# Splitting the spectrum straight from its PSUM bank, shrinking in the bank of the mix, and moving the lower part of y to GpSimd

## The chip, the cores and the metric

The kernel runs on one core of a Trainium2 chip. The metric is device time in microseconds of one execution; the table below gives the runs of the kernel before, and one further execution was taken with the profiler. Engines are named as in the profile: PE is TensorE (matmuls) and PEld its weight loads, DVE is VectorE, ACT is ScalarE, POOL is GpSimd, SP is SyncE, which here issues the DMAs.

## The reference, cut to what matters

```
X  = rfft(x, axis=1)                       # x: 8 x 3008 x 256
Yr = Xr @ w_r - Xi @ w_i + b_r
Yi = Xr @ w_i + Xi @ w_r + b_i
Yr, Yi = sign(Y) * max(|Y| - 0.01, 0)      # soft shrink, each part
y  = irfft(Yr + 1j*Yi, n=3008, axis=1)
g  = y @ w_gate; h = g * sigmoid(g) * (y @ w_val)   # 256 -> 1536
out = h @ w_out                                      # 1536 -> 256, 24064 rows
```

## The kernel before, in words

The kernel has two stages. `transform` does the Fourier transform, the complex mix of the channels, the shrink and the inverse transform for 8 batches; `gated_ffn` does the gated feed-forward net over 24064 rows in 24 blocks.

The transform of 3008 points is factored into 47 x 64. `stage_a` (L290 to L302) is the length-47 part: a chunk of x times the constant `wa`, copied out of PSUM by ACT (L298) and stored to DRAM as `d1`; there are 16 chunks to a batch. `stage_b` (L304 to L320) is the length-64 part for a pair p of the 24 rows k1 that are computed, 12 pairs to a batch and 96 in all: it loads `a_in` from `d1`, makes the spectrum in the PSUM bank `ps_b` (L311), and gives it to the mix as two parts. Every fp32 operand of the products in question is split into an upper part `hi`, rounded to the type `fp32r` of the matmuls, and a lower part `lo`, what is left of it; the list `PASSES` multiplies hi*hi, hi*lo and lo*hi. In `stage_b` ACT copies the bank to the tile `f` (real and imaginary part, L315), POOL adds the two as a third column block (L316), DVE rounds all three to `f_hi` (L318) and subtracts to get `f_lo` (L319).

`stage_mix` (L322 to L356) does the complex product with three real products: six matmuls of the sum go to the bank `ps_s` (L329), DVE adds them and the bias into the bank `mixb` of this pair (L331), and twelve more matmuls accumulate on that bank (L337). There are two `mixb` banks, used in turn. Then ACT copies the bank to the tile `t` in four pieces, which also moves the real and imaginary half to other partitions (L349), DVE clamps t to plus and minus 0.01 (L350), POOL subtracts that from t (L351), ACT rounds to `y_hi` (L354) and DVE makes `y_lo` (L355). `stage_bi` (L358 to L373) is the length-64 inverse: three matmuls into `ps_z` (L365, L368), an ACT copy to `z` (L370) and a store to `d2`. `stage_ai` (L382 to L396) is the length-47 inverse, four columns m at a time, into the banks `ps_x0` and `ps_x1`, copied by ACT (L395) and stored to `xt_d`. `load_seven` and `load_weights` (L213 to L257) turn the weights of the net into the seven operands of a Strassen-like scheme, on DVE, POOL and ACT, between the other work.

All eight PSUM banks are in use, one buffer to each name: `ps_a`, `ps_b`, `ps_s`, `ps_z`, `ps_x0`, `ps_x1` and the two `mixb`.

The order of the work comes from slots. The kernel puts a step of the work in a numbered slot with `at` and emits the slots in turn:

```
            at(s, lambda b=b, p=p: fs.__setitem__((b, p), stage_b(b, p)))
            at(s + 1, lambda b=b, p=p: ys.__setitem__((b, p), stage_mix(b, p, fs.pop((b, p)))))
            at(s + 2, lambda b=b, p=p: stage_bi(b, p, ys.pop((b, p))))
```

with s the running number of the pair. The order emitted is a priority only: a planner in the framework, which simulates the program with a cost for each instruction, fixes the queue of every engine when the program is built, and each engine then takes its queue strictly in that order. Loads are bound by `paced` to come after the newest load of `a_in` on SP. At the end of the transform's 96 pairs the net begins: `x_sum` (L500, POOL, four differences for the block) and `x_part` (L506, ACT rounds to the upper part, POOL subtracts for the lower) prepare block 0, and from there the order of the net is written out by hand and not planned.

Of the kernel before, what the change touches and what calls it, by code (L numbers as in the profile page):

```python
# [145 lines left out]
def transform(ctx, tc, front, last, ps_, xp, w_r, w_i, cb, wup_raw, wdn_raw, ca, cf, ci, co, wdn, wup_d, xt_d, d2):  # L146
# [143 lines left out]
    def stage_a(b, ch, xt):  # L290
        if ch == 0:
            d1[b] = dram.tile([NK, P, C], F32, name="d1", tag="d1")
        tag = "absz"[ch % 4] if b == 0 else "a"
        ps = ps_.tile([P, T], F32, name="ps_a", tag="ps_" + tag)
        nc.tensor.matmul(ps[:96], lhsT=wa, rhs=xt, start=True, stop=True)
        tag = "azt"[ch % 3] if b == 0 else "a"
        a = sb.tile([96, T], F32, name="a", tag=tag)
        nc.scalar.copy(a, ps[:96])  # L298
        store = nc.sync.dma_start(d1[b].rearrange("k (q m) c -> (k q) (m c)", m=NM)[:, ch * T : (ch + 1) * T], a)
        if b == 0 and ch == NCH - 1:  # L300
            gates.append(store)


    def stage_b(b, p):  # L304
        t = sb.tile([P, 2, C], F32, name="a_in", tag="a_in", bufs=3)
        gates.append(nc.sync.dma_start(t, d1[b][2 * p : 2 * p + 2].rearrange("k p c -> p k c")))
        ps = ps_.tile([P, T], F32, name="ps_b")
        for cc in range(2):
            for k in range(2):
                s = (cc * 2 + k) * P  # L310
                nc.tensor.matmul(ps[:, s : s + P], lhsT=t[:, k, cc * P : (cc + 1) * P], rhs=wf[:, 2 * p + k, :], start=True, stop=True)  # L311
        f = sb.tile([P, 3 * C], F32, name="f", tag="f", bufs=2)
        hi = sb.tile([P, 3, 2, P], F32R, name="f_hi", tag="f_hi")
        lo = sb.tile([P, 3, 2, P], F32R, name="f_lo", tag="f_lo")
        nc.scalar.copy(f[:, : 2 * C].rearrange("p (q a b) -> p a q b", q=2, b=64), ps.rearrange("p (a q b) -> p a q b", q=2, b=64))  # L315
        nc.gpsimd.tensor_tensor(f[:, 2 * C :], f[:, :C], f[:, C : 2 * C], op=ALU.add)  # L316
        flat = lambda x: x.rearrange("p q a b -> p (q a b)")
        v.tensor_copy(flat(hi), f)  # L318
        v.tensor_tensor(flat(lo), f, f32(flat(hi)), op=ALU.subtract)  # L319
        return hi, lo  # L320

    def stage_mix(b, p, parts):  # L322

        mixb = mixed[p % 2]
        p1 = ps_.tile([P, T], F32, name="ps_s")
# [1 line left out]
        for cc in range(2):  # L327
# [3 lines left out]
        v.tensor_tensor(  # L331
            mixb.rearrange("p (a c) -> p a c", c=C), p1[:, :C].rearrange("p (a c) -> p a c", a=1).to_broadcast([P, 2, C]), bias[0], op=ALU.add
        )
        for half, (q, i) in enumerate(((1, 2), (0, 1))):
            for cc in range(2):
                for w, x in PASSES:
                    nc.tensor.matmul(  # L337
                        mixb[:, half * C : (half + 1) * C],
                        lhsT=parts[x][:, q, cc, :],
                        rhs=wmix[i][w][:, cc, :],  # L340
                        start=False,
                        stop=(cc, w) == (1, 1),
                        skip_group_check=True,
                    )
        t = sb.tile([P, T], F32, name="t", tag="t", bufs=2)
        y = sb.tile([P, T], F32, name="y", tag="y", bufs=2)
        for k in range(2):
            for half in range(2):
                nc.scalar.copy(t[64 * half : 64 * half + 64, k * C : (k + 1) * C], mixb[64 * k : 64 * k + 64, half * C : (half + 1) * C])  # L349
        v.tensor_scalar(y, t, LAM, -LAM, op0=ALU.min, op1=ALU.max)  # L350
        nc.gpsimd.tensor_tensor(t, t, y, op=ALU.subtract)  # L351
        hi = sb.tile([P, T], F32R, name="y_hi", tag="y_hi")
        lo = sb.tile([P, T], F32R, name="y_lo", tag="y_lo")
        nc.scalar.copy(hi, t)  # L354
        v.tensor_tensor(lo, t, f32(hi), op=ALU.subtract)  # L355
        return hi, lo  # L356

    def stage_bi(b, p, parts):  # L358
# [52 lines left out]
    for b in range(B):  # L411
        base = NP * b
        for p in range(NP):
            s = base + p
            at(s, lambda b=b, p=p: fs.__setitem__((b, p), stage_b(b, p)))
            at(s + 1, lambda b=b, p=p: ys.__setitem__((b, p), stage_mix(b, p, fs.pop((b, p)))))
            at(s + 2, lambda b=b, p=p: stage_bi(b, p, ys.pop((b, p))))
    for k in range((B - 1) * NCH):
        b, ch = k // NCH + 1, k % NCH
        s = k / X_RATE if k < X_FAST else X_FAST / X_RATE + (k - X_FAST) * (X_END - LEAD - X_FAST / X_RATE) / ((B - 1) * NCH - X_FAST)  # L420
# [24 lines left out]
    paced(load_mix)  # L445
    paced(load_inverse)
    for s in sorted(slots):
        if s < B * NP + 2:
            for fn in slots[s]:
                fn()  # L450
        gates += stores
# [1 line left out]

    def finish():
        for s in sorted(slots):
            if s >= B * NP + 2:
                for fn in slots[s]:
                    fn()

# [3 lines left out]
def gated_ffn(ctx, tc, front, ring, ps_, co, wdn, wup_d, xt_d, d2, out):  # L463
# [33 lines left out]
            at += n  # L497
        xs[blk] = {}

    def x_sum(blk, o, a, b):  # L500
        f = lambda i: raws[blk][:, i, :]
        g.tensor_tensor(f(o), f(a), f(b), op=ALU.subtract)

    SUMS = ((4, 0, 1), (6, 2, 4), (5, 2, 0), (7, 3, 6))

    def x_part(blk, n_):  # L506
        h = BLOCKS[blk][1]
        src = raws[blk][:, X_AT[n_], :]
        part = xs[blk][n_] = sb.tile([P, 2, T], F32R, name="x_parts", bufs=12)
        act.copy(part[:, 0, :h], src)  # L510
        g.tensor_tensor(part[:, 1, :h], src, f32(part[:, 0, :h]), op=ALU.subtract)  # L511

    def product(o, weights, parts, start, stop):

# [222 lines left out]
    load_x(0)  # L737
    for k in range(RING - 1):
        load_unit(k)
    for sums_ in SUMS:  # L740
        x_sum(0, *sums_)
    for n_ in X_AT:
        x_part(0, n_)

    nc.tensor.matmul(b3, lhsT=wdn[0][:, 0, 0, :], rhs=xs[0][1][:, 0, :], start=True, stop=True)
    yield
# [72 lines left out]
```

## Time and profile before

| | us |
|---|---|
| runs: median (lowest to highest of 3) | 2745.8 (2737.93 to 2747.36) |
| profiled execution, whole | 2740.56 |
| its span, first to last instruction | 2738.8 |
| PE busy in the span | 2655.4 (97%) |
| DVE, ACT, POOL busy in the span | 2087.3, 1712.2, 2061.7 |

The span is 1.8 us shorter than the profiled execution. The first 42 us load x and do `stage_a` of batch 0, from 42 to 672 us the transform is in its steady course, 672 to about 692 us is the passage to the net, and the rest is the net. A busy PE in these tables has the latency of a matmul in it (a 128x256 product is listed at some 0.28 us while they follow one another every 0.12 us), so idle PE time is a lower bound of what a stall costs. A row of a group of instructions has its line, engine, operation, tile names and shapes, its count, its busy time and mean, and behind it the idle time of its engine just before these instructions with what ended that idle time.

### The profile page before, as it was taken

To read this page: it belongs to the slowest core of one execution; us is meant where nothing else is said; L and a number is where in the kernel's file an instruction comes from. 1 tells how busy PE (TensorE), PEld (TensorE's weight loads), DVE (VectorE), ACT (ScalarE), POOL (GpSimd) and SP (SyncE) were. 2 spreads that over 40 slices of the span, in tenths; PEclk is the share of its full clock that TensorE was granted. 3 is DMA by queue.
4 is the path that set the end of the run, shared out by engine and by line. 5 is a ranking of instruction groups with operands and counts; after the bars stand their busy time and mean duration, and the time that the engine had idled before them with its cause. 6 is when DMAs were issued, how large, how long until landed. Compare 5 with 4: busy or idle time off the path is not lost. (4 is left out here: it accounts for less than half of the span.)

```text
span 2738.8 us, 39634 instructions
## 1 busy us (share of the span) xinstructions
PE 2655.4 (97%) x13173; PEld 2207.0 (81%) x13173; DVE 2087.3 (76%) x2916; ACT 1712.2 (63%) x3280; POOL 2061.7 (75%) x1574
## 2 busy tenths in 40 slices
PE   8989998989999999999999999999999999999998
PEld 5777787778788888888888888888888888888898
DVE  3776677775778777887787877787778877888787
ACT  4666666666566666666666666666665666666665
POOL 1454465564888888888888888888888888888885
PEclk9999999999999999999999999999999999999999
DMA  8889898766354444444454444444454444444453
GB/s 251 256 271 294 283 293 267 229 197 203 137 172 156 156 141 164 168 155 157 140 171 161 150 156 149 170 156 157 140 172 156 162 144 146 154 164 153 146 185 105
DMA packets 180124, 491.88 MB, mean 180 GB/s; under 512 B 17264, under 2 KB 89584, under 8 KB 179824
## 3 DMA queue, kind: packets, MB, share of 16 engines
q1 hardware_dynamic: 179920, 489.35, 54.0%
q8 instruction: 105, 1.72, 0.3%
q14 instruction: 99, 0.81, 0.1%
HBM read 378.65 MB, written 110.62 MB: 179 GB/s over the span
## 5 line engine op out<-in xcount | busy, mean ns | idle before, releaser
L516 PE MATMUL bank<-x_parts,wup 128*128 128x512 f32 (+1 forms) x6048 | 1518.2, 386 | 1.2 <-POOL x_parts L511 0.7
L516 PEld LDWEIGHTS bank<-x_parts,wup 128*128 128x128 f32 x6048 | 1125.8, 188 | 226.5 <-DVE bank L645 5.4
L536 POOL TENSOR_TENSOR h_parts<-more,h_parts 128x512 fp32r<-128x512 f32 (+1 forms) x573 | 847.6, 1492 | 113.9 <-ACT h_parts L532 99.8
L536 POOL TENSOR_TENSOR h_parts<-hidden,h_parts 128x512 fp32r<-128x512 f32 (+1 forms) x432 | 565.1, 1316 | 204.0 <-ACT h_parts L532 164.5
L516 PE MATMUL bank<-h_parts,wdn_hi 128*128 128x512 f32 (+1 forms) x2016 | 613.5, 385 | 0.9 <-POOL h_parts L536 0.9
L532 ACT CAST h_parts<-hidden 128x512 fp32r<-128x512 f32 (+1 forms) x432 | 265.0, 613 | 451.3 <-DVE hidden L618 451.3
L516 PEld LDWEIGHTS bank<-h_parts,wdn_hi 128*128 128x128 f32 x2016 | 378.2, 188 | 74.1 <-POOL h_parts L536 1.8
L618 DVE TENSOR_TENSOR hidden<-hidden,bank 128x512 f32<-128x512 f32 (+1 forms) x576 | 376.0, 674 | 77.6 <-PE bank L516 69.2
L557 DVE TENSOR_TENSOR sums<-sums,bank 128x512 f32<-128x512 f32 (+1 forms) x360 | 241.9, 672 | 245.1 <-PE bank L516 245.1
L516 PE MATMUL bank<-h_parts,wdn_lo 128*128 128x512 f32 (+1 forms) x1008 | 388.6, 386 | 4.2 <-DVE sums L557 4.2
L532 ACT CAST h_parts<-more 128x512 fp32r<-128x512 f32 (+1 forms) x576 | 351.4, 610 | 41.8 <-DVE more L527 31.3
L616 ACT ACTIVATE hidden<-bank 128x512 f32<-128x512 f32 (+1 forms) x432 | 252.2, 584 | 117.6 <-PE bank L516 117.2
L527 DVE TENSOR_TENSOR more<-hidden 128x512 f32<-128x512 f32 (+1 forms) x288 | 293.0, 1056 | 0.0
L527 DVE TENSOR_TENSOR more<-hidden,more 128x512 f32<-128x512 f32 (+1 forms) x288 | 258.6, 898 | 0.0
L351 POOL TENSOR_TENSOR t<-t,y 128x512 f32<-128x512 f32 x96 | 133.4, 1389 | 136.6 <-DVE y L350 136.6
L645 DVE TENSOR_TENSOR bank<-hidden,bank 128x512 f32<-128x512 f32 (+1 forms) x288 | 197.0, 684 | 45.0 <-PE bank L516 32.2
L623 ACT COPY bank<-bank 128x512 f32<-128x512 f32 (+1 forms) x288 | 161.6, 561 | 109.4 <-DVE hidden L618 104.0
L516 PEld LDWEIGHTS bank<-h_parts,wdn_lo 128*128 128x128 f32 x1008 | 189.5, 188 | 40.8 <-issue 4.5
L511 POOL TENSOR_TENSOR x_parts<-xf,x_parts 128x512 fp32r<-128x512 f32 (+1 forms) x168 | 209.9, 1268 | 11.5 <-PE bank L516 7.1
L316 POOL TENSOR_TENSOR f<-f 128x256 f32<-128x256 f32 x96 | 85.3, 889 | 146.0 <-ACT f L315 142.9
L631 ACT COPY hidden<-bank 128x512 f32<-128x512 f32 (+1 forms) x288 | 167.6, 582 | 2.6
L349 ACT COPY t<-mixb 64x256 f32<-64x256 f32 x384 | 140.6, 366 | 29.6 <-PE mixb L337 20.1
(94 smaller groups left out, 3273.3 us busy)
## 6 DMA issues: line engine op xcount, KB each, us to landing
wup<-wup_d SPq DMA_DIRECT2D x288, 896.0 KB, 4.6
d<-a SPq DMA_DIRECT2D x128, 192.0 KB, 4.2
a_in<-d SPq DMA_DIRECT2D x96, 256.0 KB, 4.5
out<-o SPq DMA_DIRECT2D x88, 256.0 KB, 6.1
scratch<-xp SPq DMA_DIRECT2D x116, 192.0 KB, 4.6
d<-z SPq DMA_DIRECT2D x84, 256.0 KB, 3.8
z_in<-d SPq DMA_DIRECT2D x56, 384.0 KB, 5.1
xt_d<-xt SPq DMA_DIRECT2D x56, 376.0 KB, 4.4
```

The lines of the kernel that those rows point to most:

```text
L349: nc.scalar.copy(t[64 * half : 64 * half + 64, k * C : (k + 1) * C], mixb[64 * k : 64 * k + 64, half * C : (half + 1) * C])
L511: g.tensor_tensor(part[:, 1, :h], src, f32(part[:, 0, :h]), op=ALU.subtract)
L516: nc.tensor.matmul(o, lhsT=weights[w], rhs=parts[x], start=start and i == 0, stop=stop and i == 2, skip_group_check=True)
L527: v.tensor_tensor(at(o, h), at(a, h), at(b, h), op=ALU.subtract)
L532: act.copy(pair[i][:, 0, :h], at(i, h))
L536: eng.tensor_tensor(pair[i][:, 1, :h], at(i, h), f32(pair[i][:, 0, :h]), op=ALU.subtract)
L557: v.tensor_tensor(o, o, spare[:, :h], op=ALU.add)
L616: act.activation(at(i, h), src, AF.Silu)
L618: v.tensor_tensor(at(i, h), at(i, h), src, op=ALU.mult)
L623: act.copy(b3[:, :h], b1[:, :h])
L631: act.copy(m5, b2[:, :h])
L645: v.tensor_tensor(b2[:, :h], m5, b3[:, :h], op=ALU.add)
```

## The change

In `stage_b` the upper part of the spectrum is rounded by ACT from the bank itself, DVE subtracts it from the bank for the lower part, the sum of real and imaginary part is made by an ACT copy of one and a DVE addition of the other out of the bank (tile `f`, now 256 columns), and ACT and DVE split that sum. POOL's addition is gone. `f_hi` and `f_lo` have three buffers in place of two. `stage_mix` is cut in two: `stage_sum` has the six matmuls of the sum and the addition of the bias, one slot after `stage_b`; `stage_mix` has the twelve matmuls and the shrink, one slot later, and `stage_bi` follows one slot later again. DVE clamps and subtracts in the bank `mixb`, ACT copies the shrunk result out and rounds it, and POOL makes `y_lo`. For batch 0 `stage_a` takes six names of tiles with two buffers each in place of three. Before the net, block 0's differences are made by DVE, the first part's split is emitted ahead of them, and DVE makes three of the seven lower parts.

```diff
--- before.py
+++ after.py
@@ -293,7 +293,7 @@
         tag = "absz"[ch % 4] if b == 0 else "a"
         ps = ps_.tile([P, T], F32, name="ps_a", tag="ps_" + tag)
         nc.tensor.matmul(ps[:96], lhsT=wa, rhs=xt, start=True, stop=True)
-        tag = "azt"[ch % 3] if b == 0 else "a"
+        tag = ("a", "z", "t", "y", "y_hi", "y_lo")[ch % 6] if b == 0 else "a"
         a = sb.tile([96, T], F32, name="a", tag=tag)
         nc.scalar.copy(a, ps[:96])
         store = nc.sync.dma_start(d1[b].rearrange("k (q m) c -> (k q) (m c)", m=NM)[:, ch * T : (ch + 1) * T], a)
@@ -309,17 +309,23 @@
             for k in range(2):
                 s = (cc * 2 + k) * P
                 nc.tensor.matmul(ps[:, s : s + P], lhsT=t[:, k, cc * P : (cc + 1) * P], rhs=wf[:, 2 * p + k, :], start=True, stop=True)
-        f = sb.tile([P, 3 * C], F32, name="f", tag="f", bufs=2)
-        hi = sb.tile([P, 3, 2, P], F32R, name="f_hi", tag="f_hi")
-        lo = sb.tile([P, 3, 2, P], F32R, name="f_lo", tag="f_lo")
-        nc.scalar.copy(f[:, : 2 * C].rearrange("p (q a b) -> p a q b", q=2, b=64), ps.rearrange("p (a q b) -> p a q b", q=2, b=64))
-        nc.gpsimd.tensor_tensor(f[:, 2 * C :], f[:, :C], f[:, C : 2 * C], op=ALU.add)
-        flat = lambda x: x.rearrange("p q a b -> p (q a b)")
-        v.tensor_copy(flat(hi), f)
-        v.tensor_tensor(flat(lo), f, f32(flat(hi)), op=ALU.subtract)
+
+        total = sb.tile([P, 2 * P], F32, name="f", tag="f", bufs=2)
+        hi = sb.tile([P, 3, 2, P], F32R, name="f_hi", tag="f_hi", bufs=3)
+        lo = sb.tile([P, 3, 2, P], F32R, name="f_lo", tag="f_lo", bufs=3)
+        both = ps.rearrange("p (a q b) -> p a q b", q=2, b=64)
+        first = lambda x: x[:, :2].rearrange("p q c (k b) -> p (c k) q b", b=64)
+        blocks = lambda x: x.rearrange("p (a b) -> p a b", b=64)
+        flat = lambda x: x[:, 2].rearrange("p c a -> p (c a)")
+        nc.scalar.copy(first(hi), both)
+        nc.scalar.copy(blocks(total), both[:, :, 0])
+        v.tensor_tensor(blocks(total), blocks(total), both[:, :, 1], op=ALU.add)
+        v.tensor_tensor(first(lo), both, f32(first(hi)), op=ALU.subtract)
+        nc.scalar.copy(flat(hi), total)
+        v.tensor_tensor(flat(lo), total, f32(flat(hi)), op=ALU.subtract)
         return hi, lo
 
-    def stage_mix(b, p, parts):
+    def stage_sum(b, p, parts):
 
         mixb = mixed[p % 2]
         p1 = ps_.tile([P, T], F32, name="ps_s")
@@ -331,6 +337,11 @@
         v.tensor_tensor(
             mixb.rearrange("p (a c) -> p a c", c=C), p1[:, :C].rearrange("p (a c) -> p a c", a=1).to_broadcast([P, 2, C]), bias[0], op=ALU.add
         )
+        return parts
+
+    def stage_mix(b, p, parts):
+
+        mixb = mixed[p % 2]
         for half, (q, i) in enumerate(((1, 2), (0, 1))):
             for cc in range(2):
                 for w, x in PASSES:
@@ -344,15 +355,15 @@
                     )
         t = sb.tile([P, T], F32, name="t", tag="t", bufs=2)
         y = sb.tile([P, T], F32, name="y", tag="y", bufs=2)
+        v.tensor_scalar(y, mixb, LAM, -LAM, op0=ALU.min, op1=ALU.max)
+        v.tensor_tensor(mixb, mixb, y, op=ALU.subtract)
         for k in range(2):
             for half in range(2):
                 nc.scalar.copy(t[64 * half : 64 * half + 64, k * C : (k + 1) * C], mixb[64 * k : 64 * k + 64, half * C : (half + 1) * C])
-        v.tensor_scalar(y, t, LAM, -LAM, op0=ALU.min, op1=ALU.max)
-        nc.gpsimd.tensor_tensor(t, t, y, op=ALU.subtract)
         hi = sb.tile([P, T], F32R, name="y_hi", tag="y_hi")
         lo = sb.tile([P, T], F32R, name="y_lo", tag="y_lo")
         nc.scalar.copy(hi, t)
-        v.tensor_tensor(lo, t, f32(hi), op=ALU.subtract)
+        nc.gpsimd.tensor_tensor(lo, t, f32(hi), op=ALU.subtract)
         return hi, lo
 
     def stage_bi(b, p, parts):
@@ -413,8 +424,9 @@
         for p in range(NP):
             s = base + p
             at(s, lambda b=b, p=p: fs.__setitem__((b, p), stage_b(b, p)))
-            at(s + 1, lambda b=b, p=p: ys.__setitem__((b, p), stage_mix(b, p, fs.pop((b, p)))))
-            at(s + 2, lambda b=b, p=p: stage_bi(b, p, ys.pop((b, p))))
+            at(s + 1, lambda b=b, p=p: fs.__setitem__((b, p), stage_sum(b, p, fs.pop((b, p)))))
+            at(s + 2, lambda b=b, p=p: ys.__setitem__((b, p), stage_mix(b, p, fs.pop((b, p)))))
+            at(s + 3, lambda b=b, p=p: stage_bi(b, p, ys.pop((b, p))))
     for k in range((B - 1) * NCH):
         b, ch = k // NCH + 1, k % NCH
         s = k / X_RATE if k < X_FAST else X_FAST / X_RATE + (k - X_FAST) * (X_END - LEAD - X_FAST / X_RATE) / ((B - 1) * NCH - X_FAST)
@@ -445,7 +457,7 @@
     paced(load_mix)
     paced(load_inverse)
     for s in sorted(slots):
-        if s < B * NP + 2:
+        if s < B * NP + 3:
             for fn in slots[s]:
                 fn()
         gates += stores
@@ -453,7 +465,7 @@
 
     def finish():
         for s in sorted(slots):
-            if s >= B * NP + 2:
+            if s >= B * NP + 3:
                 for fn in slots[s]:
                     fn()
 
@@ -497,18 +509,18 @@
             at += n
         xs[blk] = {}
 
-    def x_sum(blk, o, a, b):
+    def x_sum(blk, o, a, b, eng=g):
         f = lambda i: raws[blk][:, i, :]
-        g.tensor_tensor(f(o), f(a), f(b), op=ALU.subtract)
+        eng.tensor_tensor(f(o), f(a), f(b), op=ALU.subtract)
 
     SUMS = ((4, 0, 1), (6, 2, 4), (5, 2, 0), (7, 3, 6))
 
-    def x_part(blk, n_):
+    def x_part(blk, n_, eng=g):
         h = BLOCKS[blk][1]
         src = raws[blk][:, X_AT[n_], :]
         part = xs[blk][n_] = sb.tile([P, 2, T], F32R, name="x_parts", bufs=12)
         act.copy(part[:, 0, :h], src)
-        g.tensor_tensor(part[:, 1, :h], src, f32(part[:, 0, :h]), op=ALU.subtract)
+        eng.tensor_tensor(part[:, 1, :h], src, f32(part[:, 0, :h]), op=ALU.subtract)
 
     def product(o, weights, parts, start, stop):
 
@@ -737,10 +749,12 @@
     load_x(0)
     for k in range(RING - 1):
         load_unit(k)
+
+    x_part(0, 1)
     for sums_ in SUMS:
-        x_sum(0, *sums_)
-    for n_ in X_AT:
-        x_part(0, n_)
+        x_sum(0, *sums_, eng=v)
+    for n_ in list(X_AT)[1:]:
+        x_part(0, n_, v if n_ in (6, 7, 4) else g)
 
     nc.tensor.matmul(b3, lhsT=wdn[0][:, 0, 0, :], rhs=xs[0][1][:, 0, :], start=True, stop=True)
     yield
```

## Rows read from the trace of the kernel before

**Rows 1.** The page, part 1: busy time, share of the span, instructions.
```profile
PE 2655.4 (97%) x13173; PEld 2207.0 (81%) x13173; DVE 2087.3 (76%) x2916; ACT 1712.2 (63%) x3280; POOL 2061.7 (75%) x1574
```

**Rows 2.** Stages: length, then busy PE PEld DVE ACT POOL, PEclk, DMA share, GB/s.
```profile
42.00:672.00 630.00, 576.94 (x3892) 487.15 (x3891) 445.96 (x618) 411.94 (x903) 336.11 (x301) 0.98 0.80 258
350.00:400.00 50.00, 48.44 (x334) 41.00 (x333) 37.23 (x54) 34.17 (x77) 25.11 (x23) 1.00 0.94 306
```

**Rows 3.** Waits of PE and PEld, 42 to 672 us: total us, times, longest.
```profile
PE mixb L337 <- DVE mixb L331: 18.7, 22, 2.1
PE ps_z L368 <- DVE y_lo L355: 8.7, 9, 3.0
PE ps_a L295 <- ACT a L298: 6.0, 7, 3.1
PE ps_z L368 <- ACT y_hi L354: 4.1, 5, 1.6
...
PEld mixb L337 <- DVE mixb L331: 33.0, 32, 2.6
```

**Rows 4.** Timeline near 403 us: start, length, instruction.
```profile
402.92 0.28 PE L329 MATMUL ps_s<-wm_lo,f_hi 128*128 128x256 f32 x1
...
406.38 0.69 DVE L331 TENSOR_TENSOR mixb<-ps_s,bias 128x512 f32<-128x512 f32 x1
```

**Rows 5.** Groups of DVE instructions by line, 42 to 672 us.
```profile
L319 DVE TENSOR_TENSOR f_lo<-f,f_hi 128x768 fp32r<-128x768 f32 x95 | 106.5, 1121 | 1.4
L355 DVE TENSOR_TENSOR y_lo<-t,y_hi 128x512 fp32r<-128x512 f32 x94 | 78.4, 835 | 93.2 <-ACT y_hi L354 93.2
L318 DVE CAST f_hi<-f 128x768 fp32r<-128x768 f32 x94 | 75.4, 802 | 53.1 <-PE mixb L337 51.2 <-POOL f L316 1.9
L350 DVE TENSOR_SCALAR y<-t 128x512 f32<-128x512 f32 x95 | 54.7, 576 | 4.7 <-ACT t L349 4.6
```

**Rows 6.** The same lines and L331 one by one: ns min/median/max.
```profile
L319 DVE TENSOR_TENSOR f_lo<-f,f_hi x95: 942/957/2830, 41.9 to 664.8; 128x768 fp32r<-128x768 f32 x95
...
L355 DVE TENSOR_TENSOR y_lo<-t,y_hi x94: 675/692/2586, 49.9 to 668.2; 128x512 fp32r<-128x512 f32 x94
...
L318 DVE CAST f_hi<-f x94: 546/561/1893, 45.1 to 663.6; 128x768 fp32r<-128x768 f32 x94
...
L350 DVE TENSOR_SCALAR y<-t x95: 408/420/2328, 46.6 to 669.8; 128x512 f32<-128x512 f32 x95
...
L331 DVE TENSOR_TENSOR mixb<-ps_s,bias x96: 684/691/700, 41.3 to 669.2; 128x512 f32<-128x512 f32 x96
```

**Rows 7.** Groups of ACT instructions and their waits, 42 to 672 us.
```profile
L354 ACT CAST y_hi<-t 128x512 fp32r<-128x512 f32 x95 | 59.0, 621 | 58.9 <-POOL t L351 58.5
...
L315 ACT COPY f<-ps_b 128x512 f32<-128x512 f32 x94 | 55.1, 587 | 60.3 <-DVE f_lo L319 52.1 <-PE ps_b L311 4.4 <-PE ps_x L388 1.6
...
L349 ACT COPY t<-mixb 64x256 f32<-64x256 f32 x380 | 139.2, 366 | 29.2 <-PE mixb L337 19.8 <-ACT z L370 2.0 <-issue 2.0
```

**Rows 8.** Groups whose durations serve as prices, whole span.
```profile
L645 DVE TENSOR_TENSOR bank<-hidden,bank 128x512 f32<-128x512 f32 (+1 forms) x288 | 197.0, 684 | 45.0 <-PE bank L516 32.2
...
L211 DVE TENSOR_TENSOR wi_lo<-raw_i,wi_hi 128x256 fp32r<-128x256 f32 x1 | 0.4, 424 | 0.2 <-ACT wi_hi L210 0.2
...
L210 ACT CAST wi_hi<-raw_i 128x256 fp32r<-128x256 f32 x1 | 0.4, 404 | 2.9 <-DMA raw_i<-ci 2.9
```

**Rows 9.** Groups of POOL instructions, 42 to 672 us.
```profile
L351 POOL TENSOR_TENSOR t<-t,y 128x512 f32<-128x512 f32 x95 | 132.1, 1391 | 133.5 <-DVE y L350 133.5
...
L316 POOL TENSOR_TENSOR f<-f 128x256 f32<-128x256 f32 x94 | 83.8, 892 | 107.9 <-ACT f L315 104.8 <-DVE y L350 3.0
```

**Rows 10.** Timeline of the first stage: ACT's copies in stage_a of batch 0.
```profile
18.83 2.52 ACT L298 COPY a<-ps_a 96x512 f32<-96x512 f32 x5 [4.77 <-DMA d<-a]
```

**Rows 11.** Timeline of the passage to the net: the seven lower parts.
```profile
679.90 8.72 POOL L511 TENSOR_TENSOR x_parts<-xf,x_parts 128x512 fp32r<-128x512 f32 x7 [3.87 <-ACT x_parts L510]
```

**Rows 12.** One stage of the passage, columns as in rows 2.
```profile
676.70:684.00 7.30, 5.91 (x12) 3.23 (x13) 0.69 (x1) 5.22 (x10) 4.10 (x4) 0.55 0.19 63
```

## The prediction

> **What bounds the kernel now.** I read the page first, then the busy times by stage, then the waits of PE, then the groups of DVE and ACT inside the transform, and last the timeline at both ends of it. Over the whole span PE is busy for 97% [rows 1], so only what is left between its products can be won. Nearly all of that lies in the transform: from 42 to 672 us PE is busy for 576.9 of 630 us [rows 2], which leaves 53.1 us idle, or 0.55 us for each of the 96 pairs of 6.56 us. No other engine is full there: DVE 446 us (71%), ACT 412 (65%), POOL 336 (53%), and the DMA engines have a share of 0.80, though 0.94 between 350 and 400 us.
>
> The waits say what ends PE's idle time. The largest is the mix waiting for the bias that DVE adds into its bank: 18.7 us as PE shows it, 33.0 as its weight loads show it, which can't run ahead either [rows 3]. The inverse waits 8.7 us for `y_lo` and 4.1 for `y_hi`, and `stage_a` 6.0 for ACT. The timeline shows why the bias is late. The products of the sum have started by 402.92 and the last takes 0.28 us, but DVE adds the bias only at 406.38 [rows 4]: some 3.2 us in which DVE's queue did other things first. That queue holds it up twice. In one place DVE waits: 93.2 us for `y_hi` before `y_lo`, and 51.2 us for the mix to have finished reading before `f_hi` overwrites its buffer [rows 5]. In the other its own instructions take longer than they need: the four lines that the change touches have means of 1121, 835, 802 and 576 ns [rows 5], but medians of 957, 692, 561 and 420 and maxima of 1.9 to 2.8 us, while the addition of the bias, which reads a bank of PSUM, always takes 684 to 700 ns [rows 6]. The difference of means and medians is 0.70 us for a pair, 68 us in all, and it comes at random, in queues whose order is fixed.
>
> The Trainium skill, page "SBUF — State Buffer", section "Who interferes with whom", says that a DVE instruction with at most one SBUF input outside the two-port modes does not contend with GpSimd, and that one with two SBUF inputs or in such a mode does. By that rule the trace agrees: the four lines spread up to fivefold and the bias line does not.
>
> **The change, part by part.** DVE: each pair loses f_hi, f_lo, the clamp and y_lo, 3.33 us by the means [rows 5], 2.63 by the medians [rows 6]. It gains five instructions. The lower part of 512 columns out of the bank and the clamp out of the bank I price at 0.69 us each (the bias line [rows 6]), the subtraction in the bank at 0.68 (L645), the addition and the lower part of 256 columns at 0.42 each (L211) [rows 8]: 2.91 us. By the means that is 0.42 us less for a pair, 40 us of DVE time over 96 pairs; by the medians 0.28 us more, 27 us in all. I take the means, because the time now lost to the spread is in the execution and only one short instruction of the new five (the 256-column lower part) reads two SBUF tiles.
>
> The Trainium skill, page "VectorE: DVE Perf Modes", section "Why PSUM operands drop a tier", speaks against the change: an operand in PSUM caps an fp32 instruction at one element a cycle, while the clamp in SBUF may run at two. The medians bear that out (420 ns for the clamp, 691 for the bias out of PSUM), and by it alone DVE would get slower by those 27 us rather than faster by 40.
>
> ACT: the copy of the whole bank stays (587 ns [rows 7]), and two instructions of 256 columns are added, 404 ns each by the nearest row [rows 8], 0.81 us for a pair and 78 us in all. ACT goes from 412 to 490 us, 78% of the stage: off the path on average, but it also empties `ps_a`, `ps_z` and `ps_x`, so I let the 6.0 us that PE waits for it double: +6. ACT also loses two waits of its own, 58.5 us for POOL's `t` and 52.1 for the buffer of `f` [rows 7].
>
> POOL: it loses 1.39 and 0.89 us for a pair [rows 9] and gains `y_lo` at about 1.25 (8.72 over seven [rows 11]): 1.0 us less. POOL is not on the path; its worth is that it disturbs DVE less.
>
> The split of the mix: the bias is now due a slot (6.56 us) ahead of the twelve products, and neither `y_lo` nor the wait for `y_hi` stands ahead of it on DVE. Its wait costs between 18.7 and 33.0 us [rows 3]; I take the weight loads' figure, as a product needs its load, and leave 4: -29. What I cover it with is the slot; without it, the 0.69 us of the bias is on the path again. What is queued behind the bias on DVE is the spectrum's split of the next pair. The bank `mixb` is held a slot longer, but there are two, and from the bias to the end of the copies I count a slot, clamp, subtraction and copies (6.56 + 0.69 + 0.68 + 1.46 = 9.4 us) and the products, of the 13.1 that two pairs give.
>
> From mix to inverse the chain was four copies at 366 ns, clamp 576, POOL 1391, rounding 621 and y_lo 835 [rows 5, 7, 9], 4.9 us; it becomes clamp 691, subtraction 684, copies, rounding and 1.25 us on POOL: 4.7. Its length stays; what goes is that y_lo stands in DVE's queue. Of the 12.8 us of `y_lo` and `y_hi` I take 8 off.
>
> The bank `ps_b` was freed by one ACT copy (587 ns); now ACT's two and DVE's two have to be done, 587 + 404 + 424 + 691 = 2.1 us with no queueing. The next pair needs it a pair's 6.56 us later, less its own eight products. From nothing to 0.5 us a pair (48 us) I take +3, near the low end, since the copy alone already starts late without stopping PE for it.
>
> Batch 0: ACT waits 4.77 us for a store to free a buffer [rows 10]. Twice the buffers remove that wait; the copies behind it still have to be made and stored on the same queue. Between 0 and -4.8 I take -2. SP's queue keeps its order: stores and then loads.
>
> The passage: POOL makes the seven lower parts in 8.72 us [rows 11] while PE waits for them; with three on DVE it needs four, 3.7 us less. From 676.7 to 684 us PE's granted clock is 0.55, near its lower level of 1.2 GHz, [rows 12]; its products then take longer than the parts need, so a little of it is lost: -3. The four differences (earlier, out of PE's way) count nothing. One slot more at the end: the chain of the last pair is as long as before, but with less beside it: +2.
>
> **Sum.** -29 - 8 + 6 + 3 - 2 - 3 + 2 = -31 us against the profiled execution's 2740.6: 2709.6, so **2710 us**. The median of the runs is 5.2 above that execution; I don't carry this over, as the runs themselves differ by 9.4. The net after 692 us is unchanged: same queues, written out by hand.
>
> **Rivals.**
> *The wait only changes its name* (no change). Slots are priorities and the planner has already put the sum's products 3.5 us ahead of the bias [rows 4], so the split may give it little that is new; DVE's time goes up by the medians, ACT's to 78%, and PE waits for ACT's copies of `a`, `z` and the spectrum as long as it did for the bias. For it: ACT would become the fullest engine after PE. Against it: 145 us of waits in DVE's queue and 110 in ACT's have their cause removed. Time: -29 and -8 are given back by ACT, only the start, the passage and the drain are left: about 2738. Chance 0.18.
> *The bank of the spectrum* (slower). With four readers on two engines, `ps_b` comes free too late as soon as the queueing of ACT and DVE between them comes near 6.56 - 2.1 = 4.4 us; DVE's lower part behind a long instruction of the weights can do that. If PE then waits 0.6 us for every pair, that is +58 on -31: about 2767. Chance 0.09.
> *All idle time goes.* If DVE's queue was behind all of PE's waits, the 53.1 us go, and the 4.8 at the start: about 2683. Against it: the DMA share of 0.94 where PE is already busy for 48.4 of 50 us [rows 2]; that part can't give much. Chance 0.11.
> *The change does not do what it says* can hardly be: the instructions are moved by name from one engine to another.
>
> **How the numbers follow.** The forecast itself gets 0.62. About 0.5% (13.7 us) is what a measurement of this kernel can tell from no change. The forecast's terms are good for about 12 us each way, so nearly all of it and the third rival count as faster: 0.71. The first rival and the forecast's weak end give 0.20 for the same, the second 0.09 for slower. The range reaches from the third rival, 2684, to just beyond the first, 2742; the second lies outside.
>
> **What would show it.** Right: in the steady stage, PE's wait for L331 near nothing, PE idle under 30 us over the same work, DVE's lines out of PSUM with hardly any spread, ACT at about 78%, no DVE wait for `y_hi`, and the whole stage shorter by some 28 us; at the start no wait of ACT for a store; in the passage four lower parts on POOL and three on DVE. Wrong: PE waiting for ACT's copies or for `ps_b` by tens of us, the DMA share at its full in most slices, or an equal length of the stage with other names in its waits.

## The result and the profile after

The changed kernel takes 2715.26 us (median, 2709.34 to 2722.38), against 2744.99 for the kernel before in the same set of runs. The ratio is 0.9905 with an interval of 0.9886 to 0.9924, so 29.7 us are gone. The profiled execution took 2714.87 us, 25.7 less than the one before.

The two spans are best compared between three marks: the first product into `ps_b`, the last product into `mixb`, and the first product of the net into the bank of block 0.

| us | before | after | difference |
|---|---|---|---|
| start: to the first product into `ps_b` | 35.0 | 31.6 | -3.4 |
| steady: from there to the last product into `mixb` | 637.4 | 614.3 | -23.1 |
| drain: from there to the net's first product | 7.5 | 8.6 | +1.1 |
| net: the rest | 2058.9 | 2058.6 | -0.3 |
| span | 2738.8 | 2713.1 | -25.7 |

Nearly all of it comes from the steady stage. These are the busy times of that stage, first in the kernel before, then in the kernel after (columns as in [rows 2]):

```profile
35.00:672.40 637.40, 583.74 (x3922) 492.15 (x3922) 450.22 (x625) 415.28 (x909) 337.57 (x303) 0.98 0.81 258
```

```profile
31.63:646.15 614.52, 579.02 (x3908) 494.51 (x3909) 403.03 (x724) 466.90 (x1098) 217.63 (x203) 0.97 0.83 267
```

PE is busy for 579 us of it, 584 before; what shrank most is the idle time, from 53.7 to 35.5 us. ACT has become the fuller helper (467 us, 76%), DVE is down from 450 to 403 and POOL from 338 to 218. The waits of PE and of its weight loads in the kernel after, which answer to [rows 3]:

```profile
PE ps_x L399 <- DMA z_in<-d: 18.3, 13, 3.5
PE mixb L348 <- DVE mixb L337: 3.7, 5, 1.5
PE ps_b L311 <- DVE f_lo L323: 3.5, 5, 1.0
PE ps_x L399 <- ACT xt L406: 3.0, 3, 1.9
PE ps_b L311 <- issue: 2.7, 3, 1.8
PE ps_a L295 <- ACT a L298: 1.0, 1, 1.0
```

```profile
PEld ps_x L399 <- DMA z_in<-d: 24.6, 15, 3.7
...
PEld mixb L348 <- DVE mixb L337: 11.4, 17, 1.9
```

The wait for the bias fell from 18.7 to 3.7 us (33.0 to 11.4 by the weight loads), the waits for `y_lo` and `y_hi` are gone from PE's list, and the wait for ACT's copy of `a` fell from 6.0 to 1.0. The wait that grew most is that of the length-47 inverse for its load `z_in`, 18.3 us by PE and 24.6 by the weight loads; before it was:

```profile
PE ps_x L388 <- DMA z_in<-d: 9.4, 10, 2.1
...
PEld ps_x L388 <- DMA z_in<-d: 7.5, 6, 2.3
```

The bank of the spectrum grew as well, from 0.9 us to 3.5 and 2.7. A line with `issue` is time in which PE waited for nothing that the profile shows.

DVE's waits in the kernel after:

```profile
DVE f L322 <- ACT f L321: 92.6, 52, 4.6
DVE y L358 <- PE mixb L348: 46.2, 40, 5.0
DVE f_lo L325 <- ACT f_hi L324: 26.2, 28, 3.3
```

The waits for `y_hi` and for the mix to release `f_hi` [rows 5] are gone, but these three are longer together than those two were.

DVE's new instructions one by one (ns minimum/median/maximum), which answer to [rows 6]:

```profile
L322 DVE TENSOR_TENSOR f<-f,ps_b x95: 403/420/423, 38.8 to 636.2; 128x256 f32<-128x256 f32 x95
L323 DVE TENSOR_TENSOR f_lo<-ps_b,f_hi x95: 675/683/691, 39.1 to 636.6; 128x512 fp32r<-128x512 f32 x95
L325 DVE TENSOR_TENSOR f_lo<-f,f_hi x95: 406/425/1789, 39.7 to 638.3; 128x256 fp32r<-128x256 f32 x95
L358 DVE TENSOR_SCALAR y<-mixb x96: 675/686/693, 43.5 to 646.2; 128x512 f32<-128x512 f32 x96
L359 DVE TENSOR_TENSOR mixb<-mixb,y x96: 681/689/700, 44.8 to 646.9; 128x512 f32<-128x512 f32 x96
```

The four that read a bank of PSUM spread by 20 ns at most. The one that reads two tiles of SBUF still reaches 1.8 us. Which of them contend with POOL is what the Trainium skill, page "SBUF — State Buffer", section "Who interferes with whom", states, and the trace agrees on both sides of it (the overlaps with POOL's instructions are in the last section).

### The profile page after: what moved, and what is told of

The parts are those of the page before. It is cut to its first block, busy times and chain, and to the rows that moved or that the text cites. A ratio compares the mean times of both kernels' runs of the same rounds, so it can differ in the third digit from the quotient of the medians.

```text
span 2713.1 us, 39929 instructions
## 1 busy us (share of the span) xinstructions
PE 2649.8 (98%) x13173; PEld 2211.8 (82%) x13173; DVE 2043.8 (75%) x3019; ACT 1765.6 (65%) x3472; POOL 1939.9 (72%) x1471
## 5 line engine op out<-in xcount | busy, mean ns | idle before, releaser
L366 POOL TENSOR_TENSOR y_lo<-t,y_hi 128x512 fp32r<-128x512 f32 x96 | 125.8, 1311 | 351.7 <-ACT y_hi L365 311.5
L399 PEld LDWEIGHTS ps_x<-wo,z_in 96*128 96x128 f32 x896 | 115.0, 195 | 41.5 <-DMA z_in<-d 24.6
```

## The experiments

In every run the net took 2058.0 to 2059.4 us, so the steady stage carries most of the differences; it is given for each run from its one profile, with PE's idle time in it, beside the ratio to the kernel before from the timed runs. Before: 637.4 us, idle 53.7; the changed kernel: 614.3, idle 35.5. One profile is a coarse measure: PE's busy time in the stage moves between 569 and 593 us, at granted clocks of 0.99 and 0.96, and a kernel whose stage is unchanged (the two ends alone, below) had 641.3 us, 3.9 more than before.

**The split of the mix alone** (with the third buffer it needs).

```diff
+        hi = sb.tile([P, 3, 2, P], F32R, name="f_hi", tag="f_hi", bufs=3)
...
+    def stage_sum(b, p, parts):
...
+            at(s + 1, lambda b=b, p=p: fs.__setitem__((b, p), stage_sum(b, p, fs.pop((b, p)))))
+            at(s + 2, lambda b=b, p=p: ys.__setitem__((b, p), stage_mix(b, p, fs.pop((b, p)))))
+            at(s + 3, lambda b=b, p=p: stage_bi(b, p, ys.pop((b, p))))
```

> The kernel before with the split of the mix alone: stage_sum one slot ahead of stage_mix, and the third buffer of f_hi and f_lo that it needs; the instructions of DVE, ACT and POOL are as before. Of the 23 us that the change takes from the steady stage (first product into ps_b to last into mixb): if the slot is what frees PE from the wait for the bias, this alone gives 15 to 25 us and PE's wait for the bias falls from 18.7 to under 6 us. If DVE's queue is what holds the bias up (its waits for y_hi and the spread of its instructions), the planner had already put the sum's products ahead and this gives under 8 us.

Ratio 0.9991 (0.9982 to 1.0), steady 632.7 us, idle 46.2. The slot alone gives next to nothing: 4.7 us of the stage, hardly more than two profiles of one stage differ. PE's waits in this run:

```profile
PE ps_z L373 <- DVE y_lo L360: 14.0, 17, 1.4
PE mixb L342 <- DVE mixb L331: 8.8, 10, 3.2
```

The wait for the bias was halved, and the wait for `y_lo`, behind the same full queue of DVE, grew from 8.7 to 14.0 in its place (and to 5.4 at the inverse's first product, L370, where it was 0.8).

**The third buffer alone.**

```diff
-        hi = sb.tile([P, 3, 2, P], F32R, name="f_hi", tag="f_hi")
+        hi = sb.tile([P, 3, 2, P], F32R, name="f_hi", tag="f_hi", bufs=3)
-        lo = sb.tile([P, 3, 2, P], F32R, name="f_lo", tag="f_lo")
+        lo = sb.tile([P, 3, 2, P], F32R, name="f_lo", tag="f_lo", bufs=3)
```

> The kernel before with three buffers of f_hi and f_lo and nothing else. If DVE's 51.2 us of waiting for the mix to release f_hi is what makes the bias late, this alone gives over 10 us and that wait goes. If the slot or the moved instructions are the cause, it gives under 5 us, and DVE's wait only changes its name.

Ratio 0.9988 (0.9978 to 0.9997), steady 632.3 us, idle 50.3: as much as with the slot. DVE's wait for the mix went from 51.2 to 10.6 us, and a wait of `f_hi` for POOL's sum took over (28.3 us). PE's waits in this run:

```profile
PE mixb L337 <- DVE mixb L331: 19.8, 23, 2.3
PE ps_z L368 <- DVE y_lo L355: 12.5, 18, 1.4
```

The wait for the bias is as long as before (18.7), so its halving in the run above is the slot's. In time, though, the slot, without the rest, adds nothing that its buffer doesn't give.

**The split of the spectrum from its bank alone**, the hunk of `stage_b` in the change, with two buffers.

```diff
-        nc.scalar.copy(f[:, : 2 * C]...
-        nc.gpsimd.tensor_tensor(f[:, 2 * C :], f[:, :C], f[:, C : 2 * C], op=ALU.add)
...
+        nc.scalar.copy(first(hi), both)
...
+        v.tensor_tensor(first(lo), both, f32(first(hi)), op=ALU.subtract)
```

> The kernel before with the spectrum split straight from its bank alone (ACT rounds, DVE subtracts from the bank, ACT and DVE make the sum), two buffers. If DVE's queue is the cause, the 0.5 us that DVE saves per pair by the means and the end of the spread of f_hi and f_lo (1.9 and 2.8 us at most) give 8 to 15 us. If the slot is the cause, within 5 us of no change. If four readers hold ps_b too long, PE's wait for ps_b grows from 1 us to over 10 and it is slower.

Ratio 1.0065 (1.0047 to 1.0082), steady 651.6 us, idle 58.4: slower, by 14 us in the stage, of which 4.7 are idle time of PE and 9.5 a longer busy time, at a granted clock of 0.96 (0.98 before). DVE was busy for only 396 us in it, 54 less than before, and yet nothing is won. Its waits, and PE's:

```profile
DVE y L356 <- ACT t L355: 78.2, 54, 10.1
DVE mixb L337 <- PE ps_s L335: 72.0, 36, 6.0
DVE f L322 <- ACT f L321: 27.0, 39, 2.2
```

```profile
PE ps_x L394 <- DMA z_in<-d: 21.7, 15, 3.4
PE mixb L343 <- DVE mixb L337: 13.2, 15, 2.3
PE ps_a L295 <- DMA scratch<-xp: 10.0, 11, 2.3
PE ps_b L311 <- DVE f_lo L323: 5.8, 6, 1.7
```

The bias now waits at the head of DVE's queue for the sum's products, 72.0 us where it was 0.9, and the clamp for ACT's copies, 78.2 where it was 4.6. But that is not what PE is late with: its own wait for the bias fell from 18.7 to 13.2 us. What grew there are the waits for two loads, `z_in` (9.4 before) and the chunks of x for `stage_a` (not in PE's list before). `ps_b` is not it either, at 5.8 us. None of the three cases expected fits, and why the loads come later is not shown. Less work on an engine did not make a program with fixed queues any faster.

**The shrink in the bank and y_lo on POOL alone.**

```diff
+        v.tensor_scalar(y, mixb, LAM, -LAM, op0=ALU.min, op1=ALU.max)
+        v.tensor_tensor(mixb, mixb, y, op=ALU.subtract)
...
-        v.tensor_scalar(y, t, LAM, -LAM, op0=ALU.min, op1=ALU.max)
-        nc.gpsimd.tensor_tensor(t, t, y, op=ALU.subtract)
...
-        v.tensor_tensor(lo, t, f32(hi), op=ALU.subtract)
+        nc.gpsimd.tensor_tensor(lo, t, f32(hi), op=ALU.subtract)
```

> The kernel before with the shrink in the bank of the mix and y_lo on GpSimd alone. DVE no longer waits for y_hi (93.2 us before) and its clamp no longer spreads. If DVE's queue is the cause: 8 to 20 us. If the slot is the cause: under 5 us. It could also be slower, since the bank is now held through two DVE instructions and four copies, in the slot in which the next bias but one is wanted; then PE's wait for the bias grows.

Ratio 0.995 (0.9934 to 0.9965), steady 623.0 us, idle 45.3. This is the only one of the three large parts that pays by itself, by as much as the theory of DVE's queue had it: the wait for `y_hi` is gone from DVE, though DVE now waits 120.5 us for the mix instead. PE's wait for the bias is still 13.3 us, and that for `z_in` has grown:

```profile
PE ps_x L388 <- DMA z_in<-d: 16.1, 14, 3.9
PE mixb L337 <- DVE mixb L331: 13.3, 16, 2.4
```

**Each of the three undone in the changed kernel.** First the split of the mix:

```diff
-            at(s + 3, lambda b=b, p=p: stage_bi(b, p, ys.pop((b, p))))
+            at(s + 2, lambda b=b, p=p: stage_bi(b, p, ys.pop((b, p))))
...
```

> The changed kernel with the split of the mix undone: sum, bias and mix in one slot, the inverse one slot later, three buffers of f_hi and f_lo kept. If the slot is the main cause, this gives back 15 us or more of the 29.7 and PE's wait for the bias is back at 15 us or more. If DVE's queue is the cause, it gives back under 6 us.

Ratio 0.9951 (0.9937 to 0.9964), some 13 us given back; steady 636.9 us, idle 48.4, in a profiled execution of 2738.1 us, longer than the median of its runs, 2728.8. The amount lies between the two theories, and its place is in neither. PE's waits:

```profile
PE ps_x L394 <- DMA z_in<-d: 21.4, 12, 4.5
PE ps_b L311 <- issue: 8.8, 6, 2.5
PE ps_b L311 <- DVE f_lo L323: 6.4, 4, 2.3
PE mixb L343 <- DVE mixb L337: 5.3, 7, 1.5
```

The bias costs 5.3 us here, hardly more than with the slot (3.7). In company the slot hardly touches the wait for the bias (12.7 us without it by the weight loads, 11.4 with it); without it PE stands longer ahead of the products into the bank of the spectrum, 15.2 us where the changed kernel has 6.2. Of the 15.2 only 6.4 are a wait for readers of that bank; the rest has no cause that the profile shows.

Then the split of the spectrum:

```diff
-        nc.scalar.copy(first(hi), both)
...
+        nc.gpsimd.tensor_tensor(f[:, 2 * C :], f[:, :C], f[:, C : 2 * C], op=ALU.add)
...
```

> The changed kernel with the split of the spectrum undone: f copied whole by ACT, summed by POOL, f_hi and f_lo of 768 columns by DVE. If DVE's queue is the cause, 8 to 15 us are given back, and the spread of f_hi and f_lo returns; if the slot is, under 5 us.

Ratio 0.9927 (0.9908 to 0.9947), steady 622.8 us, idle 38.6: 6 us given back, though its interval overlaps with the changed kernel's. PE's wait for the bias is back at 10.8 us (19.7 by the weight loads):

```profile
PE mixb L342 <- DVE mixb L331: 10.8, 10, 3.0
```

In company the part that cost 14 us alone costs nothing, and seems worth something.

Then the shrink:

```diff
-        v.tensor_tensor(mixb, mixb, y, op=ALU.subtract)
...
+        nc.gpsimd.tensor_tensor(t, t, y, op=ALU.subtract)
...
-        nc.gpsimd.tensor_tensor(lo, t, f32(hi), op=ALU.subtract)
+        v.tensor_tensor(lo, t, f32(hi), op=ALU.subtract)
```

> The changed kernel with the shrink undone: copies to t, clamp by DVE on SBUF, subtraction by POOL, y_lo by DVE. If DVE's queue is the cause, 8 to 20 us are given back, with DVE's wait for y_hi back near 90 us; if the slot is, under 5 us.

Ratio 0.9866 (0.9848 to 0.9884), steady 601.2 us, idle 26.2: not slower but 11 us faster than the changed kernel, and the intervals don't touch. Both theories missed this. The part that pays most alone costs in company. PE's waits, and two of DVE's:

```profile
PE ps_x L399 <- DMA z_in<-d: 9.5, 10, 2.3
...
PE mixb L348 <- DVE mixb L337: 1.9, 4, 0.8
PE ps_z L379 <- DVE y_lo L366: 1.9, 5, 0.6
```

```profile
DVE y_lo L366 <- ACT y_hi L365: 59.4, 46, 2.8
DVE f L322 <- ACT f L321: 49.5, 47, 2.6
```

Here the bias is down to 1.9 us with DVE still waiting 59.4 us for `y_hi`; of that wait of DVE, which the prediction had as one of the two causes, 1.9 us reach PE as a wait for `y_lo`. And `z_in` is back at 9.5.

**The two ends alone.**

```diff
+        tag = ("a", "z", "t", "y", "y_hi", "y_lo")[ch % 6] if b == 0 else "a"
...
+    x_part(0, 1)
+        x_sum(0, *sums_, eng=v)
+        x_part(0, n_, v if n_ in (6, 7, 4) else g)
```

> The kernel before with the two ends alone: six names of tiles in the first stage, and block 0's differences and three lower parts on DVE. From the two traces I expect the first product into ps_b 3.3 us earlier and the passage within 1 us of before, 3 to 4 us in all: the passage's shorter parts are not seen because PE's products there run at the lower clock (granted 0.55) and take as long as the parts did. If the parts on POOL were the bound, the passage would be 3 us shorter and the whole 6 us.

Ratio 0.9988 (0.9977 to 0.9999), 3.3 us by it. The first product into `ps_b` starts at 31.7 instead of 35.0 us, and the net takes 2058.5 instead of 2058.9; the stage between, which this edit leaves alone, took 641.3 us with 52.8 idle, so the profile as a whole is no shorter. As expected: the start is worth some 3.3 us, the passage nothing that can be seen. The other profiles bear the start out: the nine kernels with the six names begin that product at 30.6 to 32.3 us, the five without them at 34.6 to 37.9.

**Which half of the shrink costs.** First y_lo alone back on DVE, the shrink left in the bank; then clamp and subtraction back on `t`, y_lo left on POOL.

```diff
-        nc.gpsimd.tensor_tensor(lo, t, f32(hi), op=ALU.subtract)
+        v.tensor_tensor(lo, t, f32(hi), op=ALU.subtract)
```

> The changed kernel with y_lo back on DVE, clamp and subtraction still in the bank. Undoing the whole shrink won 11 us. If y_lo on GpSimd is what costs them, this alone wins 8 us or more. If it is the shrink in the bank (ACT's copies behind two DVE instructions, 42 us of ACT's waits, with the next pair's copies behind them), this stays within 4 us of 2715 or is slower, as DVE gets 0.7 us more for each pair and waits for y_hi again.

```diff
-        v.tensor_scalar(y, mixb, LAM, -LAM, op0=ALU.min, op1=ALU.max)
-        v.tensor_tensor(mixb, mixb, y, op=ALU.subtract)
...
+        v.tensor_scalar(y, t, LAM, -LAM, op0=ALU.min, op1=ALU.max)
+        nc.gpsimd.tensor_tensor(t, t, y, op=ALU.subtract)
```

> The changed kernel with clamp and subtraction on t in SBUF as before (DVE clamps, GpSimd subtracts), and y_lo on GpSimd as changed. If the shrink in the bank is what costs the 11 us, this is as fast as undoing both, 2700 to 2709. If y_lo on GpSimd is, it is near 2715. GpSimd then has both instructions, 2.7 us of a pair's 6.3.

With y_lo on DVE: 0.987 (0.985 to 0.989), steady 608.7 us, idle 30.1. With y_lo on POOL and the shrink in SBUF: 0.9891 (0.987 to 0.9913), steady 610.1, idle 32.4. So it is y_lo on POOL: with the shrink in the bank, taking y_lo off POOL moves the ratio from 0.9905 to 0.987 (9 us, the intervals meet between 0.9886 and 0.989); with the shrink in SBUF, from 0.9891 to 0.9866 (7 us, with overlapping intervals). Neither pair is clear of its intervals alone, but the two agree. Where the shrink itself is done makes no difference that shows (0.987 and 0.9866, 0.9905 and 0.9891). It is not y_lo's own latency at PE: in the changed kernel the inverse's weight loads wait for it 1.0 us. The waits with y_lo on DVE, then those with y_lo on POOL and the shrink in SBUF:

```profile
PE ps_x L399 <- DMA z_in<-d: 11.1, 11, 2.5
...
DVE f L322 <- ACT f L321: 45.9, 32, 2.9
```

```profile
PE ps_x L399 <- DMA z_in<-d: 9.5, 11, 2.7
PE mixb L348 <- DVE mixb L337: 8.9, 6, 3.2
PE ps_b L311 <- issue: 7.7, 4, 2.2
...
DVE f L322 <- ACT f L321: 76.4, 59, 5.5
```

What goes with y_lo on POOL in both pairs is DVE's longer wait for ACT's copy of the sum: 92.6 against 45.9 us, and 76.4 against 49.5. What reaches PE differs: in the first pair it is `z_in` (18.3 against 11.1 us), in the second the bias (8.9 against 1.9) and time ahead of `ps_b` that the profile lists as `issue` (7.7 against 1.0), with `z_in` at 9.5 in both.

**The inverse one slot later after its load**, first in the changed kernel, then in the one without the shrink. The fourth buffer goes to all that shares its name, the net's weights in `load_weights` and x of batch 0 among them.

```diff
+ZLEAD = 2
...
-        at(s + LEAD, lambda b=b, u=u: stage_ai(b, u, zs.pop((b, u))))
+        at(s + ZLEAD, lambda b=b, u=u: stage_ai(b, u, zs.pop((b, u))))
...
-        t = last.tile([P, UM * C], F32, name="z_in", tag="z_in", bufs=3)
+        t = last.tile([P, UM * C], F32, name="z_in", tag="z_in", bufs=4)
```

> The changed kernel with the use of z_in two slots after its load is emitted in place of one, and four buffers of it in place of three. PE's longest wait in the changed kernel is for z_in (18.3 us by PE, 24.6 by its weight loads). If the loads come late because SP's queue and the transfer need more than one slot, the wait falls under 5 us and 8 to 18 us are won: about 2700. If the wait only passes on what another engine is late with, the gain is under 4 us and another wait takes its name.

> The changed kernel without the shrink in the bank (the fastest so far, 2704.1), with the same later use of z_in and four buffers. Its wait for z_in is 9.5 us (12.3 by the weight loads). If lateness of the load is the cause: 5 to 10 us, about 2696. If the wait only passes on other lateness: within 4 us of 2704.

In the changed kernel: 0.9925 (0.9904 to 0.9946), steady 622.9 us, idle 40.2, no gain. The wait for `z_in` fell only to 12.3 us, and the waits for the spectrum's bank, the bias and `a` grew (6.7, 6.7 and 4.2 us for 3.5, 3.7 and 1.0). So the wait for `z_in` seems mostly to pass on other lateness. In the other kernel: 0.9843 (0.9819 to 0.9866), 2698.3 us, steady 597.5, idle 28.7, the fastest kernel here; its 6 us over the 2704.1 are within the overlap of the intervals, and its wait for `z_in` did not fall (11.9 us). It beats the kernel before by 43 us and the changed one by some 17.

## Why the prediction was right, and where its reasons were not

The total was right: 2710 us were forecast, 2715.26 measured, and by the steps -31 against -25.7 us of the profiled executions. The places were right too: the steady stage was to give 28 us and gave 23.1. Of the signs named beforehand, PE idle under 30 us did not come: it is 35.5 in the changed kernel, and 26.2 only with the shrink undone.

Step by step. **The bias** was to go from 33 us to 4 by the weight loads: it went to 11.4, three quarters of the step. **The inverse** was to lose 8 of the 12.8 us for `y_lo` and `y_hi` and lost all of it, as PE shows it. **ACT's copies** were to cost 6 us more: PE waits for `a` 5.0 us less and for `xt` 3.0 more, though ACT is at 76% as forecast (78%). **The spectrum's bank** was to cost 3 us more: from 0.9 to 6.2 us with what is listed as `issue`, 5.3 more; the rival built on it, 58 us, came nowhere near in any run (15.2 at most). **DVE's price list** held by the medians: the five new instructions come to 0.42 + 0.69 + 0.42 + 0.68 + 0.69 = 2.9 us, as forecast. By the means it was too low. In the stage the five were busy for 289 us against 318 for the four lines before, 28 less and not 40, because the lower part of 256 columns, priced at 0.42 us, reads two tiles of SBUF and has a mean of 554 ns:

```profile
L325 DVE TENSOR_TENSOR f_lo<-f,f_hi 128x256 fp32r<-128x256 f32 x95 | 52.6, 554 | 26.7 <-ACT f_hi L324 26.2
```

DVE's busy time in the stage fell by 47 us all the same; much of the rest is in the weights' instructions (L223 to L232), 84 us after 99. The rule of the page "VectorE: DVE Perf Modes" of the Trainium skill, section "Why PSUM operands drop a tier", is borne out for the instruction (the clamp's median went from 420 to 686 ns) and did not decide the stage.

**A term that was missing** is `z_in`: PE's wait for it doubled, from 9.4 to 18.3 us. I named 0.80 of DMA share as no bound and asked no further what would be late next. The load itself hardly got slower, 5.4 us at the median from issue to landing (5.1 before), so it is issued late for the slot that needs it. The split of the spectrum alone (21.7 us) and the shrink with y_lo on POOL alone (16.1) each bring the longer wait; the slot (6.3) and the third buffer (3.5) do not.

**The total owes something to luck.** Against the forecast the bias was 7.4 us short, the bank of the spectrum 2.3 worse and `z_in` 8.9 worse; the inverse was 4.8 better and ACT's copies 8.0 better. These come to some 6 us, near the 5 by which the stage fell short (an estimate, as it adds waits of PE to waits of its weight loads). The errors were as large as 9 us each, and they cancelled.

**The step that failed** is the attribution, "The split of the mix: the bias is now due a slot ahead of the twelve products", which was given 29 of the 31 us. The slot alone does halve the wait for the bias, but gives 0.9991, the same as its third buffer, as the inverse waits longer for `y_lo` instead (14.0 and 5.4 us, 12.5 with the buffer alone). Undone in the changed kernel it costs 13 us, yet the wait for the bias stays at 5.3 us. There it is the split of the spectrum that goes with the bias: without it PE waits 10.8 us (19.7 by the weight loads), in the seven kernels that have it together with other parts 1.9 to 8.9 (7.2 to 13.8), from one profile each. The first rival's reason fits this (the planner had already put the sum's products ahead), though not its time. What the slot does in company is, as far as its one profile shows, to keep PE from standing ahead of the products into `ps_b`.

**A second step failed in part**: y_lo on POOL was costed as a gain, a hop taken out of DVE's queue. It takes 93.2 us of waiting for `y_hi` off DVE, and together with the shrink in the bank it is worth 14 us alone (the two were not tried apart there), but in the finished kernel it costs 7 to 9 us. DVE's waits were the wrong thing to count: 144 us of them lost their cause, and 165 us of others took their place in the changed kernel. With the shrink undone DVE is busy for 398 of 601 us and has time for its wait.

The three parts don't add. Alone they give 0.9991, 1.0065 and 0.995, with the ends 0.9988; the product is 0.9994, and the change gives 0.9905. I read this as the planner's doing, since each engine's order is drawn up anew for every kernel; no run holds the order fixed, so this is not shown. Nor is it settled how y_lo on POOL comes to delay the copy of the sum, and what of that reaches PE.

**The ends.** Start: -2 forecast, -3.4 measured, and ACT's wait for a store is gone there. Drain: +2 and +1.1. Passage: -3 and -0.3. There the mechanism was named and undersized: the four parts on POOL, three on DVE and the first products in the kernel after:

```profile
654.55 6.35 POOL L523 TENSOR_TENSOR x_parts<-xf,x_parts 128x512 fp32r<-128x512 f32 x4 [2.37 <-ACT x_parts L522]
655.12 5.16 PE L528 MATMUL bank<-x_parts,wup 128*128 128x512 f32 x12
655.55 0.84 DVE L523 TENSOR_TENSOR x_parts<-xf,x_parts 128x512 fp32r<-128x512 f32 x1 [7.93 <-ACT x_parts L522]
656.59 3.17 DVE L523 TENSOR_TENSOR x_parts<-xf,x_parts 128x512 fp32r<-128x512 f32 x2 [0.21 <-ACT x_parts L522]
```

```profile
654.53:660.45 5.92, 5.71 (x14) 3.39 (x14) 4.64 (x4) 4.26 (x9) 5.90 (x4) 0.60 0.27 90
```

The second fence is the stage's busy times (columns as in [rows 12]): PE's granted clock is 0.60 on average in this stretch, near its lower level of 1.2 GHz, after it had stood 2.25 and 0.84 us for the last `y_hi` and `y_lo`. Twelve products take 5.16 us, 0.43 each; at that rate the 21 products of seven parts would take 9.0 us (an estimate), as long as the parts took before [rows 11], so I read that parts which come sooner can't be seen. The weight loads' wait for POOL's parts did fall, from 3.3 to 1.2 us, and the net is no shorter for it. And the parts came less soon than counted: side by side, POOL's take 1.59 us each on average (1.25 before) and two of DVE's 1.59 each.

## What to carry to other kernels

When a planner or a hand fixes the order of every queue, the parts of a change don't add up: test each part alone and each part undone, as the part that pays best alone may cost in company (here 0.995 alone, and 11 us won by taking it out again). Long waits on an engine that isn't the bottleneck (93 us for `y_hi` here) are worth something only as far as they reach the engine that is. A wait that grows in place of another (`z_in` here) is not a new bound until giving its cause more time shortens the whole. And an engine's own waits say little of what the bound engine waits for: with the spectrum split alone, the bias stood 72 us in DVE's queue while PE's wait for it fell.

## What was not expected of the hardware

That DVE's instructions with at most one tile of SBUF beside a bank of PSUM would hardly spread was expected; they kept to 675 to 700 ns for 512 columns in all 95 or 96 cases. Not expected was how much is left in the one that reads two tiles of SBUF: at 256 columns it reached 1789 ns, four times its median. Laid against POOL's instructions in the trace of the changed kernel, each of the 24 of its 96 executions that took over 500 ns overlaps one of them, and 55 of the other 72 overlap none. The clamp out of the bank overlaps one in 44 of its 96 executions and never took more than 693 ns. And splitting subtractions between POOL and DVE gains less than the count: seven took 8.72 us on POOL alone and still 6.35 us when three of them went to DVE.
